# One PSUM bank per engine for the top-k compares, with a new order of all instructions, in an agent-attention and mixture-of-experts kernel

## The chip, the cores and the metric

The kernel runs on one core of one Trainium2 chip. The metric is the device time of one execution in microseconds (us), as the median of the executions that were timed. Beside it stands one execution that the hardware profiler recorded. Its engines are called TensorE (PE in the rows; PEld is its loading of weights), VectorE (DVE), ScalarE (ACT), GpSimd (POOL) and SyncE (SP, which here only starts transfers).

## What is computed

For each of 4 batches, 12608 tokens of width 128 pass through an attention over 49 agents. Then the 128 tokens with the highest gate score go through a small network and are replaced.

```python
a2k = sm(agents, k)            # softmax over tokens, 49 x 12608
agent_v = a2k @ v              # 49 x 128
q2a = sm(q, agents)            # softmax over agents, 12608 x 49
x = q2a @ agent_v              # 12608 x 128, the output before the experts
scores = einsum('bsd,d->bs', x, w_gate)
for b in range(4):
    top_idx = argpartition(-scores[b], 128)[:128]
    xe = x[b, top_idx]
    ye = maximum(xe @ w1, 0) @ w2            # w1 128 x 1024, w2 1024 x 128
    g = 1 / (1 + exp(-scores[b, top_idx]))
    out[b, top_idx] = xe + g * ye
```

## The kernel before

A batch lies on 128 partitions with 99 tokens on each, cut into seven chunks (`CHUNKS`: six of 15 columns, one of 9). For each batch b and chunk c the program records these steps, each under a tag:

- `k`: load a chunk of keys, compute scores (`S`) on TensorE, transpose them (`sk`) and take maxima (`mx`) on VectorE. `kmax` joins the maxima. `exp` subtracts on GpSimd and takes the exponential on ScalarE. `v` loads the values and `av` adds up the products on TensorE in one PSUM bank.
- `fin`: scale the sum and make from it the small matrix `ws` (`W` in the code) that every later product of this batch needs.
- `q`, `qe`, `turn`, `gate`: load a chunk of queries, scores, softmax, split in two fp16 halves (`f`), transpose on TensorE (`fT`) into a stored tile `ft`, and multiply by the gate column (`pg`).
- `rank`: `q_rates` turns `pg` into scores (`scs`), and `topk` picks the 128 best tokens.
- `fill` (seven chunks of batch 0) and `out` (the chunks of batches 1, 3, 2): products `po` on TensorE from `ft` and `ws`, scaling into `og` on VectorE, or on ScalarE, or on ScalarE and GpSimd together, then the store by SyncE.
- `expert`: for the group of batches 0, 1, 2 and for batch 3 alone, GpSimd gathers the picked queries (`xq`); TensorE computes the token again (`qT`, `sc`, `eT`, `xT`, `xe`), then the two layers (`ph` with `hT`, and `py`); GpSimd writes the rows (`ey`) over the output.

`topk` (line 865) keeps the eight largest scores of each partition (`top`), which makes 1024 candidates. TensorE spreads them, 512 at a time, over all partitions into a PSUM tile `all0` and then `all1`, with four products each. Each of the eight candidates that a partition holds is then compared with both tiles. The compare with a count is one instruction, on VectorE `ge` or on ScalarE `ga`. `ONACT` gives to ScalarE the last four of the eight, so both engines read both tiles. `all0`, `all1` and the tile `pc` that adds up the counts come one after the other from the ring X, which has one bank; for the last batch `all1` comes from ring V. The rings are psS (3 banks, for `S` and part of `po`), psT (2), psO (1, for `po`), psV (1, for `av`) and psX (1, also for `pg`). `OUT_PS` gives every `po` tile ring O, until five tiles of the later chunks are done (`SOLO`); from then on O and three times S follow in turn.

The order is made by a planner in the program. `Recorder.touch` (line 164) notes on whom an instruction depends, `price` a cost, and `place` (line 281) walks through modelled time: each engine takes the ready instruction of lowest `urgency`, with a bonus `STICK` for the same kind as the last, and TensorE's instructions count as ready `SLACK` ns after the result of another engine. Each engine's queue is then issued in that order and the engine works through it in order. Urgency is a number for each tag (`RANKS`), the same for all engines that work on the tag. Waits between engines are set by the framework at issue. A model of TensorE's clock (`WINDOW`, `STAY`, `RISE`, `WORK`) also enters the planner's costs.

Of the kernel before, what the change touches and what calls it, by code (L numbers as in the profile page):

```python
# [14 lines left out]
F32 = mybir.dt.float32  # L15
F16 = mybir.dt.float16
BF16 = mybir.dt.bfloat16
# [5 lines left out]
PSUM = bass.MemoryType.PSUM  # L23
# [25 lines left out]
SLACK = 417.6  # L49
STICK = 81.27  # L50
# [4 lines left out]
ONACT = (4, 4, 4, 4)  # L55
# [52 lines left out]
class Recorder:  # L108
# [56 lines left out]
    def touch(self, op, ap, write):  # L165
# [18 lines left out]
        for q, other, w in log:  # L184
            if other is not op and (w or write) and q[0] < r[1] and r[0] < q[1] and q[2] < r[3] and r[2] < q[3]:
                op.deps.add(other.seq)
# [65 lines left out]
WINDOW, STAY, RISE = 3413.333, 0.43, 0.73  # L252
WORK = {"S": 1.0, "av": 0.89, "po": 0.75, "pg": 0.22, "fT": 0.67, "all": 0.83, "ph": 0.9}
# [30 lines left out]
def place(rec, urgency, slack=0.0, stick=0.0):  # L284
# [8 lines left out]
    rank = [(urgency(op.tag), op.seq) for op in ops]  # L293
# [13 lines left out]
    while len(order) < len(ops) or ends:  # L307
# [58 lines left out]
    "setup": 56.6,  # L366
# [5 lines left out]
    },  # L372
    "kmax": {0: -950, 1: -102, 2: 396.7, 3: 192.2},
    "exp": {
# [4 lines left out]
    },  # L379
# [5 lines left out]
    },  # L385
# [5 lines left out]
    },  # L391
    "fin": {0: 173, 1: -167.4, 2: -99.4, 3: 365.1},
# [5 lines left out]
    },  # L398
# [5 lines left out]
    },  # L404
    "turn": {
# [4 lines left out]
    },  # L410
    "gate": {
# [4 lines left out]
    },  # L416
    "rank": {0: -72.2, 1: -7.2, 2: -693.6, 3: -215.1},
    "weights": {0: 514},
    "fill": {
        0: {0: -968, 1: 998.3, 2: -291.4, 3: 24, 4: -40.2, 5: -247.2, 6: -255.6},  # L420
    },
    "out": {
# [3 lines left out]
    },  # L426
    "expert": {2: 1054.8, 3: -63.6},
# [3 lines left out]
def urgency(tag):  # L431

    r = RANKS.get(tag[0], 0.0)
    for x in tag[1:]:
        r = r.get(x, 0.0) if isinstance(r, dict) else r
    return r


def const_layout(capacity):
    nst = max(1, -(-capacity // P))  # L440
    parts = {
        "sel": (2 * A),
        "steps": ROUNDS * (CANDS + 1),
        "offs": ROUNDS * CANDS,
        "jv": COLS,
        "slot": nst,
        "prow": 1,
        "tri": P,
        "srow": nst * P,
        "pcol": 1,  # L450
        "kk": TOP,
        "under": TOP * len(ONACT),
    }
    at, pos = {}, 0
    for n, w in parts.items():
        at[n] = (pos, pos + w)
        pos += w
    return at, pos, nst


def make_consts(capacity):
# [22 lines left out]
    under = np.full((len(ONACT), TOP), capacity - 0.25, np.float32)  # L484
    for b, n in enumerate(ONACT):
        under[b, TOP - n:] -= 512.0
    c[:, slice(*at["under"])] = under.reshape(1, -1)
# [4 lines left out]
def agent_attention_moe(ctx, tc, qT, kT, va, agT, wgb, w1, w2, consts, qs, outs, capacity):  # L492
# [51 lines left out]
    def cs(name):  # L544
        return cst[:, spot[name][0]:spot[name][1]]
# [320 lines left out]
    def topk(b):  # L866
# [7 lines left out]
        side8 = TOP - ONACT[b]  # L874
        cnt = [t(f"c{h}", [P, TOP]) for h in range(2)]
        for h in range(2):
            pool, tag = (psV, "V") if h and b == B - 1 else (psX, "X")
            bk = pool.tile([P, 512], F32, tag=tag, name=f"all{h}_{b}")
# [6 lines left out]
            ge = sm.tile([P, 512], BF16, tag="ge", name=f"ge_{b}_{h}", bufs=1)  # L885
            ga = sm.tile([P, 512], BF16, tag="ga", name=f"ga_{b}_{h}", bufs=1)
            for k in range(TOP):
                if k < side8:
                    nc.vector.scalar_tensor_tensor(
                        ge, bk, top[:, k:k + 1], minus2.broadcast_to([P, 512]),  # L890
                        op0=ALU.is_gt, op1=ALU.mult, accum_out=cnt[h][:, k:k + 1],
                    )
                else:
                    nc.scalar.activation(
                        ga, bk, AF.Sign, scale=-1.0, bias=top[:, k:k + 1], accum_out=cnt[h][:, k:k + 1]
                    )
        pc = psX.tile([P, 512], F32, tag="X", name=f"pc_{b}")
        with rec.group():
# [8 lines left out]
            m[:, :TOP], pc[:, :TOP], -0.5, cs("under")[:, TOP * b:TOP * b + TOP],  # L907
# [395 lines left out]
```

## Time and profile before

| | us |
|---|---|
| median of 3 executions (lowest and highest) | 317.69 (316.83 to 318.55) |
| the profiled execution, its own time | 316.94 |
| its span, first to last instruction | 315.1 |
| TensorE busy | 272.8 |
| VectorE busy | 226.5 |
| GpSimd busy | 186.2 |
| ScalarE busy | 170.6 |
| moved by DMA | 106.69 MB, of it 26.21 MB written |

Busy times are sums over the whole span; an engine is idle where it waits for another engine, for a buffer or for a transfer. The span can be read in stages: up to 222 us the inputs are loaded, and after that only outputs are left to store. Between the span and the execution's own time lie 1.84 us.

### The profile page before, as it was taken

The numbers are of one execution on the slowest core, as the hardware profiler recorded it, in microseconds if no ns is written. First come the engines' busy times: TensorE is split into PE (matmuls) and PEld (weight loads), VectorE is DVE, ScalarE is ACT, GpSimd is POOL, SyncE is SP. The second block draws the span as 40 slices with busy tenths as digits, with TensorE's granted clock in tenths as the row PEclk, the third lists the DMA queues.
The fourth block names the chain that finished last, engine by engine and source line by source line (L and its number), as shares of the span: only waits on it lengthen the run. The fifth ranks groups of instructions, "written<-read, shape, count | busy, mean of one in ns | idle before, by whom it ended". The sixth has DMA issues, their size and how long they took to land. (4 is left out here: it accounts for less than half of the span.)

```text
span 315.1 us, 8560 instructions
## 1 busy us (share of the span) xinstructions
PE 272.8 (87%) x3524; PEld 179.1 (57%) x3524; DVE 226.5 (72%) x507; ACT 170.6 (54%) x306; POOL 186.2 (59%) x158
## 2 busy tenths in 40 slices
PE   2798879999999999998899998989987986878993
PEld 0133326456335655656656645667876886777593
DVE  1899985797988858737778879756456837899630
ACT  1026655645683533663775483986468844753320
POOL 7046399968869825255813769986443672665232
PEclk9999999999999999999999999999999997999998
DMA  7999999999999999999999999896940695687650
GB/s 286 419 412 417 416 417 419 411 414 418 415 417 410 409 424 322 415 410 348 345 378 363 418 413 361 320 355 236 284 172 2 267 407 212 252 345 320 250 210 31
DMA packets 18203, 106.69 MB, mean 339 GB/s; under 512 B 2032, under 2 KB 3440, under 8 KB 18160
## 3 DMA queue, kind: packets, MB, share of 16 engines
q1 hardware_dynamic: 17472, 105.07, 84.6%
q8 instruction: 30, 0.49, 0.6%
q0 software_dynamic: 256, 0.52, 0.5%
q10 hardware_dynamic: 432, 0.50, 0.4%
q14 instruction: 13, 0.11, 0.1%
HBM read 79.87 MB, written 26.21 MB: 337 GB/s over the span
## 5 line engine op out<-in xcount | busy, mean ns | idle before, releaser
L1224 PE MATMUL S<-xT,ag_sb 128*32 128x480 f32 (+1 forms) x896 | 101.2, 558 | 16.9 <-DMA ag_sb<-agT 6.2
L1224 POOL TENSOR_TENSOR sq<-sq,qm 128x735 f32<-128x735 f32 (+1 forms) x35 | 47.6, 1369 | 48.9 <-DVE qm L1224 47.0
L1224 PEld LDWEIGHTS <-ft 128*128 128x128 f16 x1188 | 59.7, 98 | 19.9 <-issue 18.4
L1224 PE MATMUL po<-ws,ft 128*128 128x128 f16 x792 | 56.0, 222 | 6.8 <-DVE og L1224 3.7
L1224 POOL TENSOR_TENSOR og<-og,r 128x512 f32<-128x512 f32 (+1 forms) x39 | 36.1, 943 | 37.8 <-ACT og L1224 37.7
L1224 PE MATMUL av<-v,sk 128*64 128x129 f32 x792 | 54.2, 277 | 4.0 <-DVE avs L1224 1.3
L1224 PEld LDWEIGHTS S<-xT,ag_sb 128*32 128x32 f32 x896 | 24.0, 110 | 55.8 <-issue 18.3
L1224 ACT COPY ft<-fT 128x896 f16<-128x896 f16 (+2 forms) x49 | 43.0, 895 | 22.1 <-PE fT L1224 19.3
L1224 PEld LDWEIGHTS av<-v,sk 128*64 128x64 f32 x792 | 45.7, 136 | 15.6 <-issue 6.7
L1224 POOL TENSOR_TENSOR f<-sq,f 128x735 f16<-128x735 f32 (+1 forms) x28 | 42.6, 1528 | 19.7 <-ACT f L1224 14.4
L1224 POOL TENSOR_TENSOR sk<-sk,mb 128x735 f32<-128x735 f32 (+1 forms) x28 | 46.7, 1703 | 7.6 <-DVE mb L1224 7.5
L1224 DVE STREAM_TRANSPOSE sq<-S 128x480 f32<-128x480 f32 (+1 forms) x56 | 35.3, 642 | 11.0 <-PE S L1224 10.0
L1224 ACT ACTIVATE sq<-sq,lift 128x735 f32<-128x735 f32 (+1 forms) x28 | 24.6, 887 | 30.4 <-POOL sq L1224 30.2
L1224 DVE TENSOR_REDUCE mx<-S 128x1 f32<-128x480 f32 (+1 forms) x56 | 32.9, 611 | 9.5 <-PE S L1224 9.3
L1224 DVE STREAM_TRANSPOSE sk<-S 128x480 f32<-128x480 f32 (+1 forms) x56 | 34.8, 636 | 4.8 <-PE av L1224 3.1
L1224 DVE SCALAR_TENSOR_TENSOR ge<-all,top,minus 128x512 bf16<-128x512 f32 x32 | 24.0, 750 | 16.0 <-ACT ga L1224 9.3
L1224 PEld LDWEIGHTS <-f 128*128 128x128 f16 x396 | 22.8, 98 | 21.1 <-issue 10.3
L1224 DVE TENSOR_REDUCE qm<-sq 128x15 f32<-128x735 f32 (+1 forms) x35 | 30.3, 866 | 2.9 <-ACT sq L1224 2.2
L1224 PE MATMUL fT<-idh,f 128*128 128x128 f16 x396 | 28.8, 220 | 3.0 <-POOL f L1224 1.1
L1224 ACT ACTIVATE sk<-sk 128x735 f32<-128x735 f32 (+1 forms) x28 | 22.1, 793 | 16.1 <-POOL sk L1224 16.1
L1224 ACT ACTIVATE ga<-all,top 128x512 bf16<-128x512 f32 x32 | 22.0, 687 | 13.1 <-DVE ge L1224 11.5
L1224 DVE TENSOR_TENSOR og<-po,r 128x512 f32<-128x512 f32 (+1 forms) x42 | 26.7, 656 | 2.2 <-PE av L1224 1.6
(131 smaller groups left out, 239.1 us busy)
## 6 DMA issues: line engine op xcount, KB each, us to landing
v<-va SPq DMA_DIRECT2D x24, 967.5 KB, 7.8
xT<-kT SPq DMA_DIRECT2D x24, 960.0 KB, 9.2
xT<-qT SPq DMA_DIRECT2D x24, 960.0 KB, 8.7
out<-og SPq DMA_DIRECT2D x24, 960.0 KB, 4.5
v<-va SPq DMA_DIRECT2D x4, 580.5 KB, 8.1
xT<-kT SPq DMA_DIRECT2D x4, 576.0 KB, 9.0
xT<-qT SPq DMA_DIRECT2D x4, 576.0 KB, 8.0
out<-og SPq DMA_DIRECT2D x4, 576.0 KB, 6.3
```

Of the source, the lines that this page charges most:

```text
L1224: call(*args, **kwargs)
```

## The change

Three things change.

First, `topk`: the table `ALL` replaces `ONACT`. The half h = 0 of the candidates goes to ring X and all its eight compares to VectorE; the half h = 1 goes to ring O in batches 0 to 2 and to ring V in batch 3, and all its eight compares to ScalarE. Each of the two work tiles gets its own tag (`g0`, `g1`). The constant `under` shrinks from four rows to one.

Second, the planner's notes: two instructions on different engines that use the same PSUM tile are now always ordered, also when both only read or touch different columns.

Third, the planner's numbers: `RANKS` holds one urgency for each tag and engine, on another scale, all with new values; `SLACK` goes from 417.6 to 18.4 ns, `STICK` from 81.27 to 13170.6, and the constants of the clock model change.

```diff
-SLACK = 417.6
-STICK = 81.27
+SLACK = 18.436502753594528
+STICK = 13170.561655066054
-ONACT = (4, 4, 4, 4)
+ALL = (("X", "O"), ("X", "O"), ("X", "O"), ("X", "V"))
...
         for q, other, w in log:
+            if ap.space == PSUM and other.engine != op.engine:
+                op.deps.add(other.seq)
...
-WINDOW, STAY, RISE = 3413.333, 0.43, 0.73
-WORK = {"S": 1.0, "av": 0.89, "po": 0.75, "pg": 0.22, "fT": 0.67, "all": 0.83, "ph": 0.9}
+WINDOW, STAY, RISE = 3413.333, 0.45, 0.76
+WORK = {"S": 1.0, "av": 0.89, "po": 0.93, "pg": 0.25, "fT": 0.8, "all": 0.83, "ph": 0.9}
...
-    rank = [(urgency(op.tag), op.seq) for op in ops]
+    rank = [(urgency(op.tag, op.engine), op.seq) for op in ops]
...
+    ('rank', 3): {"DVE": 1163.953, "ACT": -58113.571, "PE": 5301.564},
+    ('expert', 3): {"POOL": 22951.733, "PE": 74238.18, "DVE": -138033.187, "ACT": 84384.947},
...
-def urgency(tag):
+def urgency(tag, engine):
...
+    return RANKS.get(tag, {}).get(engine, 0.0)
...
-        side8 = TOP - ONACT[b]
-        for h in range(2):
-            pool, tag = (psV, "V") if h and b == B - 1 else (psX, "X")
-            bk = pool.tile([P, 512], F32, tag=tag, name=f"all{h}_{b}")
+        rings = {"X": psX, "T": psT, "V": psV, "O": psO, "S": psS}
+        for h, tag in enumerate(ALL[b]):
+            bk = rings[tag].tile([P, 512], F32, tag=tag, name=f"all{h}_{b}")
...
-                if k < side8:
+                if h == 0:
```

## Rows read from the trace of the kernel before

**Rows 1.** The page: busy time by engine, DMA share in 40 slices, chain that ended last.

```profile
PE 272.8 (87%) x3524; PEld 179.1 (57%) x3524; DVE 226.5 (72%) x507; ACT 170.6 (54%) x306; POOL 186.2 (59%) x158
...
DMA  7999999999999999999999999896940695687650
...
PE 8%; DVE 3%; issue 0%; ACT 0%; POOL 0%; POOLq 0%; DVEq 0%
```

**Rows 2.** Windows: from:to, length; busy (count) of PE, PEld, DVE, ACT, POOL; clock; DMA share; GB/s.

```profile
8.90:100.00 91.10, 80.69 (x901) 37.34 (x899) 76.75 (x137) 48.13 (x69) 62.60 (x44) 1.00 1.02 416
100.00:222.00 122.00, 114.09 (x1533) 73.12 (x1529) 90.86 (x213) 75.00 (x130) 74.22 (x53) 1.00 0.97 369
222.00:310.10 88.10, 75.33 (x1086) 67.99 (x1083) 57.32 (x153) 46.14 (x106) 42.70 (x46) 0.98 0.61 238
```

**Rows 3.** The same view of the late stretches.

```profile
233.50:262.00 28.50, 22.68 (x409) 21.29 (x410) 18.49 (x55) 19.11 (x44) 15.49 (x16) 1.00 0.61 245
262.00:310.10 48.10, 42.42 (x460) 37.02 (x460) 33.80 (x86) 21.41 (x54) 22.61 (x24) 0.96 0.61 248
...
262.00:277.00 15.00, 12.32 (x152) 11.45 (x153) 11.58 (x28) 10.39 (x27) 7.64 (x9) 0.89 0.57 232
```

**Rows 4.** Timeline (start, us, engine, operation): the last batch's index, its gathered rows, last store.

```profile
282.71 0.16 DVE L1224 SCALAR_TENSOR_TENSOR idx<-pc,e 128x1 uint32<-128x1 f32 x1
...
292.77 0.27 PE L1224 MATMUL qT<-idf,xq 128*128 128x128 f32 x1
...
310.69 0.97 POOL L1224 DMA_INDIRECT out<-ey,idx  x1 [0.82 <-DVE ey L1224]
```

**Rows 5.** Groups by shape, the compares: count, busy us, mean ns, idle before, releasers.

```profile
L1224 DVE SCALAR_TENSOR_TENSOR ge<-all,top,minus 128x512 bf16<-128x512 f32 x32 | 24.0, 750 | 16.0 <-ACT ga L1224 9.3 <-PE all L1224 6.4
...
L1224 ACT ACTIVATE ga<-all,top 128x512 bf16<-128x512 f32 x32 | 22.0, 687 | 13.1 <-DVE ge L1224 11.5 <-DVE iv L1224 1.1
```

**Rows 6.** Waits over the whole span: us in total, times, longest us.

```profile
ACT ga L1224 <- DVE ge L1224: 11.5, 16, 2.4
DVE ge L1224 <- ACT ga L1224: 9.3, 16, 1.1
PE po L1224 <- DVE og L1224: 3.7, 7, 1.4
...
PE po L1224 <- ACT og L1224: 3.0, 6, 0.9
```

**Rows 7.** Timeline of VectorE in the last batch's compares, first three and last.

```profile
263.80 0.75 DVE L1224 SCALAR_TENSOR_TENSOR ge<-all,top,minus 128x512 bf16<-128x512 f32 x1 [0.42 <-PE all L1224]
...
264.59 0.75 DVE L1224 SCALAR_TENSOR_TENSOR ge<-all,top,minus 128x512 bf16<-128x512 f32 x1
...
265.27 0.69 DVE L1224 TENSOR_TENSOR og<-po,r 128x512 f32<-128x512 f32 x1
...
276.90 0.08 DVE L1224 DVE_READ_ACCUMULATOR ge<-all,top,minus 128x1 f32 x1
```

**Rows 8.** Timeline of ScalarE in the same stretch, its first two compares.

```profile
265.45 0.69 ACT L1224 ACTIVATE ga<-all,top 128x512 bf16<-128x512 f32 x1 [2.43 <-DVE ge L1224]
...
266.26 0.69 ACT L1224 ACTIVATE ga<-all,top 128x512 bf16<-128x512 f32 x1
```

**Rows 9.** Timeline of TensorE: spreading the candidates of batches 2 and 3, two runs of output products.

```profile
240.01 1.16 PE L1224 MATMUL all<-idf,top 128*128 128x128 f32 x8 [2.34 <-ACT ga L1224]
...
261.92 1.84 PE L1224 MATMUL all<-idf,top 128*128 128x128 f32 x8 [2.24 <-DVE top L1224]
...
263.55 3.26 PE L1224 MATMUL po<-ws,ft 128*128 128x128 f16 x38
...
270.34 2.30 PE L1224 MATMUL po<-ws,ft 128*128 128x128 f16 x38
```

**Rows 10.** Windows again: the clock behind the wait of rows 9.

```profile
261.90:265.50 3.60, 3.58 (x27) 3.54 (x28) 3.14 (x9) 0.97 (x4) 1.83 (x2) 0.53 0.19 76
```

**Rows 11.** TensorE's output products in 150 to 165.1 us: ns min/median/max, first and last start.

```profile
L1224 PE MATMUL po<-ws,ft x38: 216/219/230, 151.2 to 163.2; 128*128 128x128 f16 x38
```

More of the change, by code (lines that the diff above doesn't have):

```diff
@@ L365 @@
 RANKS = {
-    "setup": 56.6,
[5 rows of a table removed]
-    },
-    "kmax": {0: -950, 1: -102, 2: 396.7, 3: 192.2},
-    "exp": {
[4 rows of a table removed]
-    },
[5 rows of a table removed]
-    },
[5 rows of a table removed]
-    },
-    "fin": {0: 173, 1: -167.4, 2: -99.4, 3: 365.1},
[5 rows of a table removed]
-    },
[5 rows of a table removed]
-    },
-    "turn": {
[4 rows of a table removed]
-    },
-    "gate": {
[4 rows of a table removed]
[L416 to L422, printed above, removed]
[3 rows of a table removed]
-    },
-    "expert": {2: 1054.8, 3: -63.6},
-}
-def urgency(tag):
[L433 to L436, printed above, removed]
+    ('setup', 0): {"ACT": -112998.916, "POOL": -41330.235, "DVE": -60677.881},
[7 rows of a table added]
@@ new lines @@
+    ('av', 0, 0): {"PE": 5144.545},
+    ('v', 0, 1): {"SP": -20520.697},
+    ('av', 0, 1): {"PE": 41745.014},
+    ('v', 0, 2): {"SP": -3630.195},
+    ('av', 0, 2): {"PE": -28204.714},
+    ('v', 0, 3): {"SP": -1826.223},
+    ('av', 0, 3): {"PE": -44870.335},
+    ('v', 0, 4): {"SP": -689.478},
+    ('av', 0, 4): {"PE": -6385.343},
+    ('v', 0, 5): {"SP": -461.295},
+    ('av', 0, 5): {"PE": 47815.339},
+    ('v', 0, 6): {"SP": -404.037},
+    ('av', 0, 6): {"PE": 43409.94},
+    ('fin', 0): {"DVE": -143642.174, "PE": -132722.281, "POOL": -39179.482, "ACT": -144313.857},
@@ new lines @@
+    ('exp', 1, 2): {"POOL": -22999.565, "ACT": -273703.34},
+    ('exp', 1, 3): {"POOL": -11794.752, "ACT": 50941.528},
+    ('exp', 1, 4): {"POOL": 12391.852, "ACT": -70255.562},
+    ('exp', 1, 5): {"POOL": -8726.541, "ACT": -265905.419},
+    ('exp', 1, 6): {"POOL": -45627.909, "ACT": -159584.905},
+    ('v', 1, 0): {"SP": -1531.14},
+    ('av', 1, 0): {"PE": -1215.218},
+    ('v', 1, 1): {"SP": -373.728},
+    ('av', 1, 1): {"PE": -9972.277},
+    ('v', 1, 2): {"SP": -310.085},
+    ('av', 1, 2): {"PE": -21710.746},
@@ new lines @@
+    ('v', 1, 3): {"SP": 62.286},
+    ('av', 1, 3): {"PE": 12071.459},
+    ('v', 1, 4): {"SP": 136.019},
+    ('av', 1, 4): {"PE": 5287.338},
+    ('v', 1, 5): {"SP": -331.148},
+    ('av', 1, 5): {"PE": 7526.148},
+    ('v', 1, 6): {"SP": 462.266},
+    ('av', 1, 6): {"PE": 44580.061},
+    ('fin', 1): {"DVE": 26660.225, "PE": 43064.008, "POOL": 16566.91, "ACT": -93282.39},
+    ('q', 1, 0): {"SP": -44565.332, "PE": -4859.535, "DVE": 23852.447},
+    ('qe', 1, 0): {"POOL": 15124.536, "ACT": -243205.25},
@@ new lines @@
+    ('gate', 1, 2): {"PE": -55.958},
+    ('q', 1, 3): {"SP": -4179.613, "PE": 58494.967, "DVE": -2373.113},
+    ('qe', 1, 3): {"POOL": 5979.345, "ACT": 63083.526},
+    ('turn', 1, 3): {"PE": 84641.148, "ACT": 37922.702},
+    ('gate', 1, 3): {"PE": 40191.252},
+    ('q', 1, 4): {"SP": -193.766, "PE": 4089.229, "DVE": -11759.983},
+    ('qe', 1, 4): {"POOL": -14231.203, "ACT": 58708.462},
+    ('turn', 1, 4): {"PE": 59502.369, "ACT": -20458.503},
+    ('gate', 1, 4): {"PE": 16295.63},
+    ('q', 1, 5): {"SP": -4074.203, "PE": 13692.017, "DVE": -287007.285},
@@ new lines @@
+    ('exp', 2, 0): {"POOL": -66111.983, "ACT": -39230.66},
+    ('exp', 2, 1): {"POOL": -88541.67, "ACT": -237451.304},
+    ('exp', 2, 2): {"POOL": 38512.057, "ACT": -5344.806},
+    ('exp', 2, 3): {"POOL": 38858.117, "ACT": -260869.322},
+    ('exp', 2, 4): {"POOL": -22337.074, "ACT": -36099.793},
+    ('exp', 2, 5): {"POOL": 35315.472, "ACT": 227268.549},
+    ('exp', 2, 6): {"POOL": -14192.993, "ACT": -145103.982},
+    ('v', 2, 0): {"SP": 826.16},
+    ('av', 2, 0): {"PE": 71287.632},
+    ('v', 2, 1): {"SP": 2756.396},
@@ new lines @@
+    ('av', 2, 1): {"PE": 751.013},
+    ('v', 2, 2): {"SP": 3836.167},
+    ('av', 2, 2): {"PE": -8410.981},
+    ('v', 2, 3): {"SP": 1590.995},
+    ('av', 2, 3): {"PE": -165085.13},
+    ('v', 2, 4): {"SP": 12558.199},
+    ('av', 2, 4): {"PE": -30013.683},
+    ('v', 2, 5): {"SP": 13241.924},
+    ('av', 2, 5): {"PE": 950.318},
+    ('v', 2, 6): {"SP": 16259.932},
+    ('av', 2, 6): {"PE": 19102.925},
+    ('fin', 2): {"DVE": -9435.426, "PE": -71911.958, "POOL": 17920.679, "ACT": -35823.533},
@@ new lines @@
+    ('exp', 3, 6): {"POOL": 3526.363, "ACT": -100679.891},
+    ('v', 3, 0): {"SP": 15220.629},
+    ('av', 3, 0): {"PE": 86870.334},
+    ('v', 3, 1): {"SP": 13302.6},
+    ('av', 3, 1): {"PE": 38605.521},
+    ('v', 3, 2): {"SP": 48327.671},
+    ('av', 3, 2): {"PE": 17592.711},
+    ('v', 3, 3): {"SP": 62142.71},
+    ('av', 3, 3): {"PE": 75093.632},
+    ('v', 3, 4): {"SP": 167533.723},
+    ('av', 3, 4): {"PE": 69217.956},
+    ('v', 3, 5): {"SP": 137538.404},
+    ('av', 3, 5): {"PE": -25726.755},
@@ new lines @@
+    ('gate', 3, 3): {"PE": 8057.233},
+    ('q', 3, 4): {"SP": 31342.837, "PE": 14822.799, "DVE": -11693.47},
+    ('qe', 3, 4): {"POOL": -3733.229, "ACT": -46568.403},
+    ('turn', 3, 4): {"PE": -170394.217, "ACT": -54975.49},
+    ('gate', 3, 4): {"PE": 233.896},
+    ('q', 3, 5): {"SP": -137.33, "PE": -189765.485, "DVE": -77569.558},
+    ('qe', 3, 5): {"POOL": 19290.354, "ACT": -72710.226},
+    ('turn', 3, 5): {"PE": -12908.735, "ACT": -104450.794},
+    ('gate', 3, 5): {"PE": 2483.093},
@@ L451, in const_layout @@
         "kk": TOP,
-        "under": TOP * len(ONACT),
+        "under": TOP,
     }
@@ L483, in make_consts @@
     c[:, slice(*at["kk"])] = 1.0 + np.arange(TOP, dtype=np.float32)[None]
[L484 to L487, printed above, removed]
+    c[:, slice(*at["under"])] = capacity - 0.25 - 256.0
     return c
@@ L894, in topk @@
                     nc.scalar.activation(
[L895 removed]
+                        gt, bk, AF.Sign, scale=-1.0, bias=top[:, k:k + 1], accum_out=cnt[h][:, k:k + 1]
                     )
@@ L906, in topk @@
         nc.vector.scalar_tensor_tensor(
-            m[:, :TOP], pc[:, :TOP], -0.5, cs("under")[:, TOP * b:TOP * b + TOP],
+            m[:, :TOP], pc[:, :TOP], -0.5, cs("under"),
             op0=ALU.mult, op1=ALU.is_lt, accum_out=m[:, TOP:],
```

152 lines of the change are left out of this document (149 added, 3 removed), and 68 rows, old and new, of the table RANKS.

## The prediction

> **What bounds the kernel now.** I began with the page's busy times and its slices. TensorE is busy 272.8 of 315.1 us, VectorE 226.5, and DMA is full in the first half and broken later [rows 1]. So no single engine explains the span, and I read it in stages. From 8.9 to 100 us DMA runs at a share of 1.02 and 416 GB/s, and TensorE is idle for 91.1 - 80.7 = 10.4 us. To 222 us the share is 0.97 and TensorE is busy 114.1 of 122. From 222 to 310.1 us, when only outputs are left to store, the share is 0.61 and TensorE is busy 75.3 of 88.1, so 12.8 us idle [rows 2]. A shorter stall in the first two stages lies beside a full DMA or a nearly full TensorE. The last stage has room, and what it gives up ends the program sooner. Of its 12.8 us, 5.8 lie in 233.5 to 262 us and 5.7 after 262 [rows 3].
>
> What ends last is a chain of the last batch: its compares run from 263.80 to 276.98, its index is made at 282.71, the gathered rows are turned at 292.77, and the last store starts at 310.69 [rows 4, 7]. The page's chain holds only 8% of the span on TensorE and 3% on VectorE [rows 1], that is some 35 us of the end. So a shorter compare phase is worth something only if TensorE, which has other work in these 48 us, can follow.
>
> **The compares.** There are 32 on VectorE and 32 on ScalarE [rows 5], eight and eight in a batch. After the change there are again 32 and 32 of the same shape, so busy time on both engines is unchanged, and TensorE spreads the same candidates. What goes is the alternation. VectorE waited 9.3 us for ScalarE's compares and ScalarE 11.5 us for VectorE's, 16 times each [rows 6]. In the last batch a ScalarE compare begins only when VectorE's pair on the same tile has ended: 264.59 + 0.75 = 265.34, then 265.45. VectorE's scaling of another tile at 265.27 overlaps that same ScalarE compare, and both keep 0.69 us [rows 7, 8]. So two engines reading two tiles at once cost nothing extra here, while on one tile they take turns.
>
> The last batch's phase takes 276.98 - 263.80 = 13.2 us [rows 7]. From start to start, a compare costs VectorE 264.59 - 263.80 = 0.79 us and ScalarE 266.26 - 265.45 = 0.81 us [rows 7, 8]. Eight take 6.3 and 6.5 us, side by side: 13.2 - 6.5 = 6.7 us less, if nothing else is put between. Now seven output scalings of VectorE of about 0.68 us, as the one at 265.27, lie between; if all stay, its part is 6.3 + 7 x 0.68 = 11.1 us and the gain 2.1 us. The bounds are 2.1 and 6.7. TensorE needs some of these scalings to free its banks, so neither end is likely; I take the middle, 4.5 us.
>
> Can TensorE follow? After 262 us it is busy 42.4 of 48.1 us [rows 3]. In 1.64 us of this it only ran slowly: the eight spreading products took 1.84 us against 1.16 for batch 2, and 38 output products 3.26 against 2.30 [rows 9]. The granted clock is 0.53 from 261.9 to 265.5 [rows 10], near the lower of its two levels (1.2 of 2.4 GHz), right after TensorE had stood 2.24 us for `top` [rows 9]. So 48.1 - 42.4 + 1.6 = 7.3 us can be had at most, and 4.5 fits. If the new order leaves TensorE's work as it is, the gain is cut to what its own waits on scalings free.
>
> **The ring.** `all1` of batch 2 stood 2.34 us at the head of TensorE's queue, until the last compare freed the only bank of ring X [rows 9]. In ring O it doesn't wait for that. Behind it in the queue stood output products that the end needs, but they could partly be waiting for scalings: 0 to 2.3 us, and I take 1.2. The same wait in batches 0 and 1 lies in the loading stages, covered by DMA [rows 2]; I cost it at nothing, and at under 1 us each if that cover is gone. The price of ring O: for as long as ScalarE compares (at least 6.5 us) no `po` tile of batch 0, and one in four later, has a bank. In batch 0's compare phase, 150 to 165 us, TensorE did 38 output products, five tiles, all in ring O [rows 11]. At worst all five move behind 222 us: 38 x 0.22 = 8.4 us of queue time by durations. These overlap, though: the 38 in rows 9 took 2.30 us, so 2.3 us is the row to use. At best the places are filled with other ready work, 0. I take 0, because TensorE still has idle places before 222 us, and keep 2.3.
>
> The Trainium skill speaks against this step (Perfetto Trace Analysis, section Matmuls): independent matmul groups should rotate through different PSUM banks, so that evacuating one overlaps the next. Lending ring O to compares leaves fewer banks for that. The trace shows the price of too few: TensorE's output products waited 3.7 us for VectorE's scalings and 3.0 us for ScalarE's over the whole run [rows 6]. By the row the sum keeps 0; by the rule it loses some of what it gains, which is the third rival below.
>
> **The new dependency in the planner.** It adds no instruction. The wait is in the trace already [rows 6], so it costs nothing on the chip; it lets the plan know that two readers of one tile take turns. After the compares are split, only the small steps on `pc` still meet it. Cost 0.
>
> **The new urgencies, `SLACK` and `STICK`.** They move nearly everything: TensorE's queue, which loads SyncE starts first, which scaling stands before which compare. The trace of before can't show the result. Below zero it is bounded by TensorE's idle time left after 222 us, 12.8 - (4.5 - 1.6) - 1.2 = 8.7 us (1.6 of the 4.5 come from the clock); not all can go, since each batch's chain has waits of its own, so I take -7. Above zero: an instruction placed ahead of its producer stands at the head of the queue, as the one for `top` did for 2.24 us and the one for the bank for 2.34 us [rows 9]. With 0.4 us less `SLACK` such places may become more; one more in each batch makes 4 x 2.3 = +9.2 us. I take 0, as both kinds of row stand in the trace, and keep both ends.
>
> **Sum.** 316.94 - 4.5 - 1.2 = 311.2 against the profiled execution. The median of the runs, 317.69, is 0.75 us above that execution, so I forecast a median of 312.0, and the rivals are medians too. About 0.5%, or 1.6 us, is what a measurement of this kernel can tell from no change.
>
> **Rivals.**
>
> 1. *The order also closes the gaps after 222 us.* Speaks for: 5.8 us idle in 233.5 to 262 [rows 3], while output products need only the banks. Against: the last batch's chain, whose value products and matrix lie there, has waits that no order removes. With 7 us more: 312.0 - 7 = 305.
>
> 2. *A tight queue (slower).* The place is TensorE's queue, where products follow VectorE and ScalarE by design; `SLACK` had put other work between. Price as above, 2.3 us for each time that TensorE stands. It decides from the third such place on, when 3 x 2.3 = 6.9 exceeds the 5.7 us gained. At five places: 312.0 + 11.5 = 323.5. A low clock behind such a wait, as in rows 10, adds 1.6 each time, so fewer suffice. For it: the trace has two such places even with 417.6 ns. Against: the plan now knows of the turns on one tile.
>
> 3. *Ring O takes back the gain.* By the rule above: output products lose places in the compare phases of batches 0 to 2 and come out after 222 us, 2.3 us, and the last batch's compares stay interleaved with scalings, so that 2.1 of 4.5 remain: 312.0 + 2.3 + 2.4 = 316.7, and 317.9 with nothing from batch 2. For it: five tiles used that ring in 15 us [rows 11]. Against: later `po` tiles have three other banks.
>
> 4. *The compares are hidden.* The split does what it says, but the end is TensorE's order of expert and output products, with 42.4 of 48.1 us busy [rows 3], and the freed time turns into a longer wait of the gathered rows (which were turned 10 us after the index [rows 4]): 317.7 less 0 to 1.
>
> **How the numbers follow.** Forecast 0.42, at 308 to 315, as the compare phase gives 6.7 or 2.1 and small losses elsewhere. Rival 1: 0.18, at 300 to 308. Rivals 3 and 4 together: 0.17, at 314.5 to 319, of it 0.04 faster by over 0.5%. Rival 2: 0.23, at 319 to 327. Faster is 0.42 + 0.18 + 0.04 = 0.64, same 0.13, slower 0.23. The range from 304 to 322 leaves out half of rival 1 and half of rival 2, 0.20 together; it takes in the sum with -7 and with +9.2 and comes close to that with +11.5.
>
> **What the profile after would show.** If the compare step is right, `ge` and `ga` have no waits for each other, both overlap in time, and each phase has 6.5 to 11 us; the index of batch 3 comes 3 to 6 us sooner; busy time of both engines stays at 24.0 and 22.0 us for the compares. If the ring step is right, `all1` doesn't wait for ScalarE. If rival 2 holds, TensorE's idle time grows with waits on VectorE and ScalarE, and low clocks appear in new places. Rival 3 shows as TensorE work after 222 us above 75 us; rival 4 as an early index and late `qT`. I am wrong most simply if the loading stage, which I hold fixed, gets longer or shorter with the new order of loads.

## The result

The kernel after takes 306.13 us (median of 4 executions, 303.28 to 307.49) against 317.48 for the kernel before beside it: a ratio of 0.9628 with a 95% interval from 0.9548 to 0.9707, 11.35 us less. The forecast was 5.7 us less, at 312.0; the time lies in its range, on the side of rival 1.

The profiled execution after took 303.28 us with a span of 301.5. That is 2.85 us under its median, while the one of before lies 0.54 under the median beside it. The two traces therefore differ by 13.6 us where the medians differ by 11.4. I read the traces for where the time went and the ratios for how much.

Stages of the kernel after (from:to, length; busy time with count of PE, PEld, DVE, ACT, POOL; clock; DMA share; GB/s):

```profile
8.90:100.00 91.10, 80.21 (x940) 39.16 (x936) 75.55 (x139) 49.90 (x71) 60.34 (x42) 1.00 1.00 406
100.00:222.00 122.00, 115.43 (x1600) 73.09 (x1593) 91.22 (x209) 73.40 (x131) 75.58 (x54) 1.00 0.94 362
222.00:296.60 74.60, 71.00 (x982) 65.07 (x981) 52.88 (x153) 45.16 (x105) 44.74 (x47) 0.98 0.76 305
```

They answer to [rows 2]; the last row ends where as much of the span is left as there. Counted from 222 us, the late stage fell from 88.1 to 74.6 us. TensorE's work in it fell from 75.3 to 71.0 us, with 982 matmul records in place of 1086, and its idle time from 12.8 to 3.6 us. So 9.2 of the 13.5 us are idle time of TensorE that closed, as rival 1 had it.

The first two rows are as long as before only because the windows are cut at the same times; they don't show that the loading stages ended where they did. The score products on the loaded keys and queries (`S`) show that they didn't. Before and after (ns min/median/max, first and last start):

```profile
L1224 PE MATMUL S<-xT,ag_sb x896: 402/566/1009, 6.2 to 221.2; 128*32 128x480 f32 x156, 128*32 128x288 f32 x24
```

```profile
L1424 PE MATMUL S<-xT,ag_sb x896: 402/566/1009, 6.2 to 208.3; 128*32 128x480 f32 x154, 128*32 128x288 f32 x26
```

The last of them starts 12.9 us sooner. (SyncE starts the last load of values 2.6 us sooner, at 219.14 in place of 221.78 us.)

The compares, by shape (count, busy us, mean ns, idle before, releaser), for [rows 5]:

```profile
L1424 DVE SCALAR_TENSOR_TENSOR gt<-all,top,minus 128x512 bf16<-128x512 f32 x32 | 23.7, 740 | 2.6 <-PE all L1424 2.1
...
L1424 ACT ACTIVATE gt<-all,top 128x512 bf16<-128x512 f32 x32 | 22.1, 692 | 1.9 <-PE all L1424 1.5
```

Busy times are as before, and of 9.3 and 11.5 us of waits for the other engine nothing is left. And TensorE's waits from 222 us to the end (us in total, times, longest), four in all:

```profile
PE po L1424 <- ACT og L1424: 0.6, 2, 0.4
PE fT L1424 <- ACT ft L1424: 0.5, 1, 0.5
PE po L1424 <- DVE og L1424: 0.2, 1, 0.2
```

The two of 2.3 us each that [rows 9] show, on the last compare and on `top`, are gone, and the output products, which waited 3.7 and 3.0 us over the whole run [rows 6], hardly wait here.

But the last batch's compares are not shorter. VectorE's part:

```profile
250.95 0.75 DVE L1424 SCALAR_TENSOR_TENSOR gt<-all,top,minus 128x512 bf16<-128x512 f32 x1 [0.50 <-PE all L1424]
...
252.42 0.69 DVE L1424 TENSOR_TENSOR og<-po,r 128x512 f32<-128x512 f32 x1
...
253.69 1.28 DVE L1424 TENSOR_TENSOR og<-po,r 128x512 f32<-128x512 f32 x2
...
263.89 0.08 DVE L1424 DVE_READ_ACCUMULATOR gt<-all,top,minus 128x1 f32 x1
```

From 250.95 to 263.97 are 13.0 us, against 13.2 [rows 7]. Output scalings stand between the compares, nine in all; two rows of them are shown. The compares of the two engines overlap, but the plan uses the freed time for scalings. Nearly all of the gain is there before them: the eight best scores (`MAX8`, for batches 2 and 3) come 12.7 and 12.9 us earlier than in the kernel before.

```profile
216.69 0.27 DVE L1424 MAX8 top<-scs 128x8 f32<-128x99 f32 x1
248.59 0.26 DVE L1424 MAX8 top<-scs 128x8 f32<-128x99 f32 x1
```

Before:

```profile
229.39 0.27 DVE L1224 MAX8 top<-scs 128x8 f32<-128x99 f32 x1
261.51 0.26 DVE L1224 MAX8 top<-scs 128x8 f32<-128x99 f32 x1
```

From batch 3's scores to the end of the span are 52.9 us after and 53.6 before; from batch 2's scores they are 84.8 and 85.7. So 12.7 of the 13.6 us are there at batch 2's scores already, ahead of 222 us. This is in part a swap, since other work stands behind this mark in the new order. The windows from it to the end, before and after:

```profile
229.39:315.10 85.71, 68.00 (x905) 60.92 (x905) 54.39 (x145) 43.73 (x103) 40.89 (x43) 0.97 0.55 223
```

```profile
216.69:301.50 84.81, 74.90 (x1036) 68.38 (x1036) 53.97 (x158) 48.39 (x111) 44.77 (x47) 0.96 0.72 283
```

TensorE has 6.9 us more to do there, in a stretch of nearly the same length, and is idle for 9.9 us in place of 17.7. The new order brings the scores forward and fills the end with what it put off.

So two things had to be asked: what the turns of the two engines really cost and in which batch, and what the new order does beside.

### The profile page after: what moved, and what is told of

It is laid out like the page before. It is cut to its first block, busy times and chain, and to the rows that moved or that the text cites. A ratio compares the mean times of both kernels' runs of the same rounds, so it can differ in the third digit from the quotient of the medians.

```text
span 301.5 us, 8552 instructions
## 1 busy us (share of the span) xinstructions
PE 269.3 (89%) x3524; PEld 177.9 (59%) x3524; DVE 221.3 (73%) x507; ACT 169.7 (56%) x306; POOL 186.4 (62%) x158
## 5 line engine op out<-in xcount | busy, mean ns | idle before, releaser
L1424 PE MATMUL av<-v,sk 128*64 128x129 f32 x792 | 51.2, 276 | 2.3 <-issue 1.9
L1424 PEld LDWEIGHTS av<-v,sk 128*64 128x64 f32 x792 | 44.2, 136 | 10.2 <-issue 5.3
L1424 PEld LDWEIGHTS <-f 128*128 128x128 f16 x396 | 23.6, 98 | 18.2 <-issue 10.0
L1424 PE MATMUL fT<-idh,f 128*128 128x128 f16 x396 | 29.7, 219 | 2.5 <-POOL f L1424 1.1
L1424 ACT CAST f<-sq 128x735 f16<-128x735 f32 (+1 forms) x28 | 22.2, 791 | 16.6 <-PE fT L1424 10.1
L1424 ACT ACTIVATE sk<-sk 128x735 f32<-128x735 f32 (+1 forms) x28 | 22.1, 793 | 10.8 <-POOL sk L1424 10.6
L1424 DVE SCALAR_TENSOR_TENSOR gt<-all,top,minus 128x512 bf16<-128x512 f32 x32 | 23.7, 740 | 2.6 <-PE all L1424 2.1
```

The lines of the kernel that those rows point to most:

```text
L1424: call(*args, **kwargs)
```

## Experiments on the turns

Each run is a ratio to the kernel before on the same chip; the medians of before beside them were 316.49, 317.76, 317.09 and 316.65 us in four groups.

**Turns away, order kept.** VectorE copies each spread tile into SBUF ahead of its first compare, and ScalarE's compares read the copy. Every queue keeps its order; eight copies of 0.69 us come in.

```diff
+            cp = sm.tile([P, 512], F32, tag="cp", name=f"cp_{b}_{h}", bufs=1)
...
+    for b in range(B):
...
+            op.calls = [(nc.nc.vector.tensor_copy, (cp, bk), {})] + list(op.calls)
+            for k in range(4, TOP):
...
+                act.calls = [(nc.nc.scalar.activation, (ga, cp, AF.Sign),
...
```

> The order of before stays, instruction for instruction; only the taking of turns goes. VectorE copies each spread tile to SBUF ahead of its first compare (8 copies of about 0.6 us), and ScalarE's 32 compares read the copy, so the two engines no longer meet in one PSUM bank. The waits of ge and ga for each other (9.3 and 11.5 us in before) should be gone. Theory 'order' (the gain of the change comes from the new urgencies, the compares were worth little): 314.5 to 318, that is 0 to 3 us below the 317.5 of before. Theory 'turns' (turn taking stood TensorE's queue in the compare phases of batches 2 and 3 and cost more than the 4.5 us of the prediction): 306 to 311. The prediction's own term would give 312 to 314.

Measured: 307.99 us, 0.9736 (0.9666 to 0.9806), 8.5 us less. The compares, by shape:

```profile
L1237 DVE SCALAR_TENSOR_TENSOR ge<-all,top,minus 128x512 bf16<-128x512 f32 x32 | 23.7, 741 | 0.4
L1237 ACT ACTIVATE ga<-cp,top 128x512 bf16<-128x512 f32 x32 | 23.1, 720 | 3.3 <-DVE cp L1237 3.0
```

VectorE's 16.0 us of idle time at the compares [rows 5] are down to 0.4; another 5.3 us stand ahead of the copies, 4.3 of them for the spreading products, where the compares had waited 6.4 for these. So the turns alone cost more in the old order than the whole forecast gain, even with 5.5 us of copies paid on VectorE.

**Is it the turns, or the bank that comes free sooner?** The copy also ends ScalarE's hold on ring X. Here ScalarE's last compare of each tile reads PSUM again (`range(4, TOP - 1)` above), so the bank comes free with the same instruction as before.

> The kernel without turns in the order of before gains 8.5 us by two things: the engines no longer wait for each other at each compare, and ring X comes free earlier for the second tile. Here ScalarE reads the copy for three of its four compares and PSUM for the last, so ring X is held until that last compare, and each tile has one turn instead of some four. If the turns are what counts: 6 to 8 us less than before (308.5 to 310.5). If the bank's release is what counts: 0 to 3 us less (313.5 to 316.5).

Measured: 310.51 us, 0.9769 (0.9725 to 0.9813), 7.3 us less, which isn't clear of the 8.5 (the intervals overlap). So the gain doesn't need ScalarE to leave the bank to the copy. But the bank came free sooner here too, because that last compare did. The products that spread batch 2's second tile:

```profile
234.96 1.16 PE L1237 MATMUL all<-idf,top 128*128 128x128 f32 x8 [0.53 <-ACT ga L1237]
```

They start 8.2 us behind batch 2's scores (226.72), as with the full copy (8.3) and not as before (10.6), and wait 0.53 us in place of 2.34 [rows 9]. The run doesn't part the turns from the wait for the bank that they cause.

**Which batch?** The copy in one batch alone (`for b in (0,)` and so on).

> The order of before, with the turns taken away in batch 0 alone (150 to 165 us, where the DMA share is 0.97): ScalarE's eight compares of batch 0 read a copy in SBUF that VectorE makes (2 copies). Theory 'covered' (the prediction's step: in the loading stage a shorter stall lies beside a full DMA and is worth nothing): no difference to before within 0.3%, that is 315.5 to 317.5. Theory 'carried' (the loads follow TensorE's queue, so what that queue gains at 150 us is still there at the end): 1.5 to 2.5 us less than before, 314 to 315.

> The kernel before, its order unchanged; in batch 1 alone VectorE copies each of the two spread score tiles to SBUF ahead of its first compare, and ScalarE's compares read the copy, so that the two engines no longer take turns there. Theory A (a turn in a batch whose phase lies beside full DMA is covered, as the prediction costed it): 0 to -1 us. Theory B (turns are paid wherever the compare phase stands on the path of TensorE's queue, and batch 1's phase ends just as the loading gets thinner): the parts sum to the -8.5 us of all four batches, of which batch 0 gave -1.0, batch 2 -4.1 and batch 3 about -2, which leaves -1 to -2 us for batch 1.

> The same in batch 2 alone (233 to 248 us, loads done, DMA share 0.33). The prediction gave this phase 1.2 us (0 to 2.3) for the wait of the second tile's products. Theory 'carried', from the milestones of the kernel without turns (the last batch's scores came 3.6 us earlier against batch 2's scores): 3 to 4.5 us less than before, 312 to 313.5. Theory 'order': under 1.5 us less.

> As the run with batch 1 alone, in batch 3 alone. The prediction's step put -4.5 us here, with bounds of -2.1 and -6.7, because the last batch's compare phase is followed by nothing but TensorE's own work. The run that split batch 3 by tiles gave -2.1 us. Theory A (that run lost some to its moved products and 16 products at a low clock; the turns themselves are worth the predicted amount): -4 to -5 us. Theory B (the scalings that stand between the compares in VectorE's queue hold the phase, so the lower bound is the real one): -1.5 to -2.5 us.

| copy in | us | ratio, interval | us against before |
|---|---|---|---|
| batch 0 | 316.73 | 0.9985 (0.9946 to 1.0024) | -0.5 |
| batch 1 | 315.88 | 0.9960 (0.9918 to 1.0003) | -1.3 |
| batch 2 | 314.59 | 0.9870 (0.9811 to 0.9930) | -4.1 |
| batch 3 | 315.01 | 0.9915 (0.9874 to 0.9955) | -2.7 |
| all four | 307.99 | 0.9736 (0.9666 to 0.9806) | -8.4 |

The last column is (ratio - 1) x 317.5. The four sum to 8.6, so within their intervals the turns add up, batch by batch. Batches 0 and 1, which lie beside the loads, are within the error of nothing by these times. The traces say more, since every queue keeps its order. From batch 0's scores to batch 1's and from there to batch 2's, before:

```profile
146.63:192.55 45.92, 42.49 (x564) 25.36 (x568) 36.74 (x90) 29.22 (x52) 27.68 (x20) 1.00 0.99 387
192.55:229.39 36.84, 34.36 (x533) 26.95 (x533) 24.38 (x65) 25.09 (x49) 27.29 (x22) 1.00 0.87 302
```

With the copies in all four batches:

```profile
146.25:190.17 43.92, 41.62 (x564) 24.48 (x560) 37.52 (x93) 29.13 (x52) 27.66 (x20) 1.00 1.01 409
190.17:225.57 35.40, 34.09 (x533) 26.90 (x533) 25.47 (x66) 25.17 (x49) 27.27 (x22) 1.00 0.87 305
```

The same 564 and 533 products take 2.0 and 1.4 us less, and the last load of values starts 3.8 us sooner (217.97 for 221.78). A DMA share of 0.99 was not a limit here: about the same 18 MB moved at 409 GB/s in place of 387. The next stretch, to batch 3's scores, is 3.6 us shorter and the rest 1.4. With the copy in batch 0 or batch 1 alone, batch 2's scores come 1.1 and 2.8 us sooner (228.25 and 226.60; in the runs with the copy in batch 2 or 3 alone they stay at 229.33 and 229.41). But the spans of these two traces are only 0.1 and 1.6 us shorter, so part of it is lost again behind that mark.

Batch 2 is worth most. With the copy in it alone the scores of batch 3 come 3.3 us sooner:

```profile
229.33 0.27 DVE L1237 MAX8 top<-scs 128x8 f32<-128x99 f32 x1
258.22 0.26 DVE L1237 MAX8 top<-scs 128x8 f32<-128x99 f32 x1
```

That is 28.9 us from batch 2's to batch 3's scores, against 32.1 before. VectorE's last compare of batch 2 starts at 242.72 in place of 245.30 us; whatever stands behind in the three queues, the steps of batch 3 among it, moves up.

**The prediction's step itself: the last batch split by tiles.** All eight compares of the first tile on VectorE, all of the second on ScalarE, in the same slots, with the second tile's four products drawn up behind the first's.

```diff
...
+    first, second = ([x for x in order if x.label == comps[b, h, 0][0].tensor.name and x.engine == "PE"] for h in range(2))
...
+    order.remove(second[0])
+    order.insert(order.index(first[0]) + 1, second[0])
```

> The order of before, with the prediction's main term alone: in batch 3 the second tile's spreading products stand right behind the first's, VectorE keeps the first tile (ring X) and ScalarE the second (ring V), in the same slots of their queues. Batches 0 to 2 are as before. The prediction's term says 4.5 us (2.1 to 6.7) less than the 317.5 of before: 311 to 315. Theory 'order': 0 to 2 less, because the scalings between the compares stay where they are and TensorE's order sets the end. Theory 'turns': 3 to 6 less, the rest with batch 2.

Measured: 314.63 us, 0.9933 (0.9896 to 0.9971), 2.1 us less by the ratio; with the copy it was 2.7. VectorE's first compare and the end of its last:

```profile
262.83 0.75 DVE L1239 SCALAR_TENSOR_TENSOR ge<-all,top,minus 128x512 bf16<-128x512 f32 x1 [0.63 <-PE all L1239]
...
273.67 0.08 DVE L1239 DVE_READ_ACCUMULATOR ge<-all,top,minus 128x1 f32 x1
```

The phase is 10.9 us, 2.3 shorter than 13.2: the lower bound of the prediction (11.1 us, 2.1 less), where all scalings stay between.

## Experiments on the order

**The new order with the turns put back.** In batches 0, 2 and 3 four compares of each engine change tiles in their slots, so both engines read both tiles again there. (In batch 1 the two engines' compares lie apart in time in the new order.)

```diff
+    for b in (0, 2, 3):
+        for k in range(4):
+            k0, k1 = (2 * k + 1, k + 4) if b == 2 else (k + 4, k)
...
+            dve.calls = [(nc.nc.vector.scalar_tensor_tensor, (gt0, bk1, top[:, k1:k1 + 1], minus2.broadcast_to([P, 512])),
...
+            act.calls = [(nc.nc.scalar.activation, (gt1, bk0, AF.Sign),
...
```

> The order of the changed kernel stays, slot for slot; in batches 0, 2 and 3 four of VectorE's and four of ScalarE's compares swap their tiles, so that both engines read both tiles again and must take turns (in batch 1 the two engines' phases lie apart in time and are left). Theory 'order': 0 to 3 us above the 306.1 of the changed kernel. Theory 'turns': 6 to 11 us above it, near before. The prediction's own term: about 4.5 us above, 310 to 311.

Measured: 309.26 us, 0.9738 (0.9676 to 0.9800). The waits of the two engines for each other (us in total, times, longest):

```profile
ACT gt L1441 <- DVE gt L1441: 6.9, 7, 2.1
DVE gt L1441 <- ACT gt L1441: 4.6, 5, 1.1
```

These are 12 waits and 11.5 us, where the kernel before has 32 and 20.8 [rows 6]; eight of the 12, 7.2 us, lie in batch 0 and one in batch 2. So there are four corners, the lower left one with about half of the turns:

| | with turns | without turns |
|---|---|---|
| order before | 1 | 0.9736 |
| order after | 0.9738 | 0.9628 |

The turns cost 2.6% in the old order, and what there is of them in the new one costs 1.1%. The new order is worth 2.6% with these turns and 1.1% without. Whether both repair the same idle time or the new order just has fewer turns to lose by, the table can't tell, so neither part has a share of its own. In the trace of this run (311.40 us, the longest of its four) batch 0's index comes 6.2 us later than in the kernel after (179.96 for 173.78), and so do batch 1's and batch 2's scores (191.22 for 185.05, 222.86 for 216.69): a stall beside the loads had not been made up by then. Over the copies alone the whole change gains 0.0108 x 317.5 = 3.4 us, and here the intervals (0.9548 to 0.9707 and 0.9666 to 0.9806) overlap.

**The parts under numbers that were not settled for them.** The split with the old urgencies (second tile in ring S, in batch 3 in ring V); the new dependency alone in the kernel before; the kernel after without the dependency; and the kernel after with the old clock constants. In each the order is planned anew. The dependency is these two lines, and the clock constants are those of the diff.

```diff
+            if ap.space == PSUM and other.engine != op.engine:
+                op.deps.add(other.seq)
```

> The split of the compares alone with the urgencies, SLACK, STICK and clock numbers of before and without the new dependency; the planner makes its order anew from them. ScalarE's tile lies in ring S in batches 0 to 2 (with ring O the old urgencies come to no order) and in V in batch 3. Theory 'order': within 3 us of before, on either side, 314.5 to 320. Theory 'turns': 6 us or more below before, 306 to 311.

> The compares, urgencies and all numbers of before; only the new dependency in the planner is added, so that its plan knows that readers of one PSUM tile on two engines take turns, and the order is made anew. Theory 'a new order costs' (the urgencies are settled for one plan, as with the split compares under the old urgencies, which took 337 us): 6 us or more slower than before, over 322. Theory 'the plan was wrong about turns' (the plan gains by knowing of them): 2 to 6 us faster, 310 to 314.

> The kernel after without the planner's new dependency between engines on a shared PSUM tile, all else the same, its order planned anew. The prediction costed the dependency at 0. Theory A (only the small steps on the counts' tile meet it, so the order hardly moves): within 1 us of the kernel after, about 306 us. Theory B (the urgencies are settled for one set of dependencies, and any other set gives an order that is not settled): 2 to 15 us slower than the kernel after, as the same dependency cost 2.5 us in the kernel before.

> The kernel after with the old constants of the planner's model of TensorE's clock, all else the same, its order planned anew. The instructions are the same, the estimated durations differ by some per cent. The prediction said nothing of these constants and so costed them at 0. Theory A: within 1 us of the kernel after. Theory B (the order is settled for these durations): 2 to 15 us slower. If TensorE's idle time after 222 us rises above 3.6 us by as much as the time, the closing of the gaps there belongs to this one settled order and not to the compares.

| | us | ratio, interval |
|---|---|---|
| split, old urgencies | 337.00 | 1.0639 (1.0579 to 1.0700) |
| before, with the dependency | 320.14 | 1.0080 (1.0037 to 1.0122) |
| after, without the dependency | 317.69 | 1.0002 (0.9959 to 1.0046) |
| after, old clock constants | 309.65 | none (306.05 to 312.42, 4 runs) |

The split without an order that suits it loses 20 us; neither theory about it had that. Two lines that add no instruction make the kernel before 2.5 us slower, which is between the two theories, and by the ratios the kernel after is 11.9 us slower without them. The run with the old clock constants decides nothing, as its times take in those of the kernel after; TensorE's idle time from 222 us is 3.8 us in it (3.6 in the kernel after), so the gaps are closed in this order too. The run without the dependency tells most. It follows the kernel after up to 222 us (TensorE 80.3 and 116.0 us busy in the two loading stages), has batch 3's scores at 251.75, and then its compares in one block:

```profile
254.88 0.75 DVE L1422 SCALAR_TENSOR_TENSOR gt<-all,top,minus 128x512 bf16<-128x512 f32 x1
...
263.00 0.08 DVE L1422 DVE_READ_ACCUMULATOR gt<-all,top,minus 128x1 f32 x1
...
271.72 0.16 DVE L1422 SCALAR_TENSOR_TENSOR idx<-pc,e 128x1 uint32<-128x1 f32 x1
```

The phase is 8.2 us in place of 13.0 and the index 0.7 us earlier than after (272.46), and yet the whole gain is lost. Early scores alone don't bring it: batch 2's are there at 216.62 us, as in the kernel after, but 97.2 us lie behind them in place of 84.8. Its TensorE from 250 to 272 us:

```profile
250.00:272.00 22.00, 17.27 (x175) 15.10 (x175) 19.62 (x58) 12.07 (x33) 5.81 (x6) 0.85 0.45 185
```

4.7 us idle and a lower clock. Output products that the kernel after has behind it run at the very end, the last eight at 301.37 us behind a wait on a scaling, where the kernel after starts its last ones at 285.07:

```profile
301.37 0.61 PE L1422 MATMUL po<-ws,ft 128*128 128x128 f16 x8 [0.84 <-DVE og L1422]
```

**Scalings or compares first?** To test that reading by itself, the kernel after gets its last batch's compares drawn together on each engine, all else in the same order (first run), or the compares and all later steps up to the index (second run).

```diff
...
+    block = [op for op in order[first + 1:] if op in [comps[B - 1, h, k] for h in range(2) for k in range(TOP)]]
+    rest = [op for op in order[first + 1:] if op not in block]
+    order = order[:first + 1] + block + rest
```

In the second run the first line has `op.tag == ("rank", B - 1) and op.engine != "SP"` as its condition.

> The kernel after, its order the same but for the last batch's 16 compares: on VectorE and on ScalarE the eight are drawn together right behind the first, so that the nine output scalings and the small steps between VectorE's compares come behind all of them. Theory A (the phase's length is on the path to the end, as the prediction had it): the phase goes from 13.0 us to about 6.5 us; the products on the counts keep their place in TensorE's queue, so the gain is small, 0 to -2 us against 306.1. Theory B (the scalings free the banks of TensorE's output products, which are the path; the phase's length is not): the first scaling comes 5 to 6 us later, TensorE stands in 252 to 262 us for 2 to 5 us with waits of the output products on the scalings, and the time is 2 to 5 us longer, 308 to 311.

> As the run with the compares drawn together, and with all later steps of the last batch's index (the transposed counts, ranks, flags, the index) drawn forward with them in the queues of TensorE, VectorE, ScalarE and GpSimd. Theory A (the last batch's chain sets the end): the index comes 5 us or more sooner than at 272.46 us and the time falls by 2 to 5 us, to 301 to 304. Theory B (TensorE's output products set the end, and the chain has slack): the index comes sooner, but TensorE now also stands for the chain's own turns with VectorE and ScalarE, 5 us or more idle in 252 to 266 us, and the time is 4 to 8 us longer, 310 to 314.

Measured: 308.62 us, 0.9757 (0.9702 to 0.9811), and 313.78 us, 0.9886 (0.9828 to 0.9943): by the ratios 4.1 and 8.2 us slower than the kernel after (by the medians 2.5 and 7.7), about what theory B said of each. The profiled execution of the first, 311.36 us, is the longest of its runs, so its rows show where the waits lie and the ratio how much they cost. TensorE in it:

```profile
253.87 1.85 PE L1430 MATMUL po<-ws,ft 128*128 128x128 f16 x30
260.16 1.01 PE L1430 MATMUL po<-ws,ft 128*128 128x128 f16 x8 [4.43 <-DVE og L1430]
...
261.60 3.41 PE L1430 MATMUL po<-ws,ft 128*128 128x128 f16 x30
```

Its window behind the stand, with all five engines:

```profile
260.00:264.00 4.00, 3.84 (x34) 3.78 (x34) 2.30 (x5) 1.97 (x5) 2.42 (x3) 0.50 0.07 31
```

VectorE's phase is 6.3 us there, from 253.18 to 259.49, the shortest that the last batch had, and TensorE stands 4.43 us for the first scaling behind it. Then it runs at a granted clock of 0.50, the lower of its two levels (1.2 of 2.4 GHz): 30 products take 3.41 us in place of 1.85. In the second run TensorE stands 5.6 us for the compares themselves and the index is there at 264.59:

```profile
260.31 0.57 PE L1430 MATMUL pc<-c,idf 128*128 128x8 f32 x2 [5.61 <-DVE gt L1430]
...
264.59 0.16 DVE L1430 SCALAR_TENSOR_TENSOR idx<-pc,e 128x1 uint32<-128x1 f32 x1
...
285.61 0.99 POOL L1430 DMA_INDIRECT xq<-q,idx  x1
```

The index is 7.9 us earlier than in the kernel after, but the gather stayed behind GpSimd's output scalings, which the stand had made late, and started 21 us after it. So this run doesn't say what an early gather would bring; it says that drawing the chain forward costs more than it frees. How much of TensorE's time goes to output products in 14 us around the phase (the view holds these products, their evacuations on VectorE and ScalarE, clock, DMA share, GB/s), first the kernel after, then the first of these runs:

```profile
250.00:264.00 14.00, 11.04 (x182) 6.48 (x11) 6.37 (x12) 1.00 0.91 373
```

```profile
250.00:264.00 14.00, 6.44 (x82) 3.79 (x6) 2.58 (x5) 0.83 0.62 256
```

Eleven scalings by VectorE and twelve by ScalarE go with 182 products; six and five go with 82. (Batch 3's scores come 2.7 us later in that execution; in 252.70 to 266.70 us its products are 81.)

## Why the prediction was right or wrong

**What bounds the kernel: right for the late stage, wrong for the loading stages.** The late stage had the room: TensorE's idle time there fell by 9.2 us. But I held the loading stages fixed, since a stall in them "lies beside a full DMA or a nearly full TensorE". This step failed, as the last sentence of the prediction feared. In the kernel after, the last score product starts 12.9 us sooner and batch 2's scores come 12.7 us sooner, though batch 0's come 5.1 us later. And with the copies, where no queue changes its order, 3.8 of the 8.8 us by which that span is shorter are gained ahead of batch 2's scores.

**The turns as the cause: right in kind, mis-sized in place.** The forecast was 4.5 + 1.2 = 5.7 us; measured are 8.5 with the order kept. With the order's 0, which measured 3.4 on top (below), this is why the whole change gained about twice what I said.

- *Last batch, 4.5 us (2.1 to 6.7).* Measured 2.1 by the split and 2.7 by the copy. I had taken the middle because TensorE needs some of the scalings between. With all of them between, the phase fell to 10.9 us; where, in the new order, it was 8.2 or 6.3, the time rose. So no run had the upper bound. It counted the compares as the path; in those two runs TensorE stood for the scalings.
- *Batch 2, 1.2 us (0 to 2.3).* Measured 4.1 (2.2 to 6.0), over three times what I took. Of the two terms in the sum this is the one that failed. I priced only the one wait in TensorE's queue [rows 9] and not the turns inside batch 2's own phase, although the same rows that I used for batch 3 [rows 5, 6] count 16 waits on each engine over four batches. That phase, too, stands after 222 us, and batch 3's scores follow it.
- *Batches 0 and 1, nothing.* Measured -0.5 (-1.7 to 0.8) and -1.3 (-2.6 to 0.1), neither clear of zero. But the cover that I gave as the reason isn't there: the stretches behind their scores are 2.0 and 1.4 us shorter without the turns. How much of this reaches the end is open.

**Ring O, 0 (to 2.3): not told apart.** TensorE's waits on scalings after 222 us are 0.8 us in all. The Trainium skill's rule (Perfetto Trace Analysis, section Matmuls), to rotate independent groups of products through PSUM banks, is borne out once here: eight products stood 0.39 us for ScalarE's last compare of batch 1, in ring O.

```profile
213.50 0.61 PE L1424 MATMUL po<-ws,ft 128*128 128x128 f16 x8 [0.39 <-ACT gt L1424]
```

Rings S, T and X weren't tried for the second tile in the kernel after.

**The new dependency, 0: wrong.** It adds nothing to the chip's work, but the plan depends on it: without it the kernel after is as slow as the kernel before. I reasoned on what it orders and not on what the urgencies were settled with.

**Urgencies, `SLACK`, `STICK`, 0 (-7 to +9.2): mis-sized.** The sign was open; measured are -3.4 over the copies alone (the two intervals overlap) and -8.3 over the kernel before with about half of the turns put back. The two waits that I counted as evidence for rival 2 vanished. The bounds held for the change as a whole; the +20 us of the split with old urgencies shows that the loss had none such.

**Rivals.** Rival 1 came true, 306.1 where it had 305, by its own mechanism: TensorE's idle time fell to 3.6 us. In the same late window with the copies alone it is 7.7:

```profile
222.00:301.40 79.40, 71.68 (x998) 65.17 (x994) 57.67 (x154) 44.32 (x104) 39.99 (x42) 0.96 0.64 256
```

I gave it 0.18, since the last batch's chain "has waits that no order removes". That was the error: the phase is still 13.0 us long, but TensorE has other work beside it. Rival 2 is what the runs off the settled order show, and the price I gave, 2.3 us for a stand and more for the clock behind it, is of the right order (4.43 us and 1.56 us in one place, 2.5 to 4.1 us in the time). Rival 3 would have shown as over 75 us of TensorE work behind 222 us; it is 71.0. Rival 4, an index that is early for nothing, is not what happened after; the second of the last two runs has an early index and a late gather, but its time also rose.

**Marks in the profile after.** No waits between the two engines, equal busy times, `all1` free of ScalarE: as said. Overlap: in batches 0, 2 and 3, but in batch 1 VectorE's compares start from 190.7 to 198.1 us and ScalarE's from 205.2 to 212.7. Phases of 6.5 to 11 us: 8.9 and 9.3 in batches 0 and 2, but 22.8 in batch 1 and 13.0 in the last. Index 3 to 6 us sooner: 10.2, as batch 3 begins 12.9 us sooner.

What stays open is which of the many moved instructions make the last 3.4 us; single moves weren't taken back one by one.

## What to carry to other kernels

Where two engines take turns on one PSUM tile, price it in every batch, not only in the last one: here the next to last was worth 4.1 us and the last 2.1 to 2.7, and the two beside the loads shortened their stretches by 2.0 and 1.4 us at a DMA share near 1. Don't hold a stage fixed because its window is: look for a mark that the work itself makes, such as the last product on loaded data. Don't count a phase as path because it is long and followed by the end; ask what stands between its instructions and who waits for that, since shortening it by pushing output scalings behind it cost 2.5 to 4.1 us. And an order that was settled for one set of dependencies and costs has to be settled again with each of them: the same instructions took from 306 to 318 us with two lines of the planner in or out.

## What the runs showed of the hardware

A copy of a 128x512 tile from PSUM to SBUF took 0.69 us on VectorE, and eight of them, 5.5 us in all, paid for themselves by 8.5 us, with four compares of ScalarE on each tile (0.72 us each from SBUF, 0.69 from PSUM) then free to run beside VectorE's. The Trainium skill (PSUM — Partial Sum Buffer, the section on PSUM bank collisions) says that two engines reading one bank at once collide and have to be ordered by semaphores; [rows 7, 8] show the order, and no run here lets such reads overlap.

A DMA share of 0.99 came with 387 GB/s in one stretch and a share of 1.01 with 409 GB/s in the same stretch without the turns, so a share near 1 did not mean that the transfers were at their limit.

A stand of 4.43 us on TensorE was followed by 4 us at a granted clock of 0.50, so that the 30 products in it alone added 1.56 us, a third of the wait, to its price. Behind the second run's stand of 5.61 us, 38 products took 3.52 us, where 38 in the kernel after took 2.30 (at 251.64).
